# Decode attention and MLP on one core: the output projection as one load at the end, last K and V whole, w4 in five pieces

## The chip, the cores and the metric

The kernel runs on one core of a Trainium2 chip. The metric is the device time of one execution in microseconds (us). Three runs of the kernel before took 404.21, 404.23 and 404.65 us; the median is 404.23 us. Beside them one execution was profiled, and the views quoted below are of that one.

## What is computed

One token (S = 1, D = 1024) goes through two blocks that work side by side, and their sum is the output. Cut to what matters:

```
xn  = layernorm(x)
A:  q = xn @ wq                      # wq 1024 x 4096: 32 heads of 128
    scores = q . k_cache / sqrt(128) # 4 KV groups, 8 heads each, 65536 keys
    o = softmax(scores) . v_cache
    a = o.reshape(4096) @ wo         # wo 4096 x 1024
B:  h  = gelu(layernorm(xn) @ w1);  hs = shift(h) @ w2   # shifted parts: zero for S = 1 (padding)
    x1 = xn + hs
    b  = x1 + gelu(layernorm(x1) @ w3) @ w4   # w3 1024 x 3584, w4 3584 x 1024
out = x + a + b
```

With one token every shifted part of h is padding, so hs is zero; the kernel still loads w1 and w2 and multiplies by them. All inputs are bf16. The K and V caches have 67 MB each, and with the weights some 170 MB are read once.

## The kernel before

**Slots.** All large inputs go through a pool of three slots (`big`, SLOTS = 3) of 128 partitions by 32768 bf16 values, 8 MB each. The list `slots` (L105 to L117) gives the order of the work: wq; then for each of the four KV groups two rounds of K and V, each load 32768 keys of one group (8 MB), with w3 after the first round; after group 2 (counted from 0) one slot with three pieces of wo and w1; after group 3 one slot with the last piece of wo, w2 and the first 10 rows of w4; and one with the other rows of w4. The last K and the last V are loaded as two halves of 4 MB into one slot, so that the first half can be worked on while the second comes. w4's 28 rows per partition are cut into pieces of 10, 7, 5, 3, 2 and 1 (W4_PIECES, L21), each with its own load.

**Order of the loads.** `issue` (L122) starts the loads of a slot, all from SyncE's queue (L128). `ensure` is called before each slot's work with a lookahead of two, so SyncE issues slot i + 2 in its list when the slot that it takes over has been consumed; SyncE waits in order, so a load that waits holds back those behind it. Loads signal their completion on a few semaphores that they take in turn, and a load that comes to one that is still in use by an earlier load waits for that load: on SyncE the first K waits for one of the small loads of x, and the first V for wq.

**Head.** ScalarE's queue loads x twice: over partitions in four parts (x_bf, L140) and as one row in three parts (x_row_bf, L144). Two layernorms follow (`layernorm`, L193 on). Four `accx` rows of 256 (L227) put x plus its normed form, which is the rest of the sum, into the PSUM row accumulator psB by `row_acc` (L184); they are the first of what is summed there. On PE the wq product (`rows_product`, L268) stands behind the matmuls of these rows.

**Attention.** `compute_K` transposes K in 32 x 32 blocks on VectorE in place (L364, four pieces for each half) and multiplies with the queries (L368); then max, exp and the transposed probabilities (L372 to L405). `compute_V` multiplies with V (L415) and rescales the running sum og (L423). After a group's last V, `group_end` (L428 to L447) masks og, sums the heads' parts by matmuls with a selector (sel8big, L434 and L436), reduces (L439, L442) and scales it into oT5, 128 x 8, one for each group.

**Row accumulator.** psB is one PSUM bank in which four strips of the PE array (32 columns apart, by tile_position) hold four quarters of the output row, 256 values each. wo (L454), w2 and w4 are all added by `row_acc`: a one-column weight and a 256-column slice of the loaded rows as the moving side, four matmuls for each row:

```
def compute_wo(g):
    for j in range(8):
        for h4 in range(4):
            row_acc(h4, oT5[:, j:j + 1], wt[:, j, QC * h4:QC * (h4 + 1)])
```

The hidden row of w3 and that of w1 go to DRAM and back from GpSimd's queue to be laid out over partitions (`bounce`, L306). After the last w4 piece ScalarE copies psB (L351) and SyncE stores the row (L352).

Of the kernel before, what the change touches and what calls it, by code (L numbers as in the profile page):

```python
# [17 lines left out]
KEYS = 16384  # L18
HALVES = 2
LOOKAHEAD = 2  # L20
W4_PIECES = (10, 7, 5, 3, 2, 1)  # L21
# [3 lines left out]
def kernel(  # L25
# [51 lines left out]
    wo_v = A_wo.rearrange("(g p j) n -> g p (j n)", g=HKV, p=P)  # L77
# [7 lines left out]
    def source(piece):  # L85
# [9 lines left out]
        if kind == "wo":  # L95
            return wo_v[piece[1]]
# [3 lines left out]
        _, g, t, parts = piece  # L100
        cache = A_k_cache if kind == "K" else A_v_cache
        v = cache[0, g, t * BK:(t + 1) * BK, :].rearrange("(p k) d -> p (k d)", p=P)
        return v if parts is None else v[:, parts * KEYS:(parts + 1) * KEYS]

    slots = [[("wq",)]]  # L105
    for g in range(HKV):
        for t in range(BIG):
            parts = range(HALVES) if (g, t) == (HKV - 1, BIG - 1) else (None,)
            for kind in ("K", "V"):
                slots.append([(kind, g, t, h) for h in parts])  # L110
            if (g, t) == (0, 0):
                slots.append([("w3",)])
        if g == HKV - 2:
            slots.append([("wo", i) for i in range(HKV - 1)] + [("w1",)])
    n4 = len(W4_PIECES)
    slots.append([("wo", HKV - 1), ("w2",), ("w4", 0)])
    slots.append([("w4", q) for q in range(1, n4)])  # L117
# [4 lines left out]
    def issue(pieces):  # L122
        t = big.tile([P, SLOT], BF16, name="slot")
        at = 0
        for piece in pieces:
# [4 lines left out]
            if piece[0] in ("K", "V"):  # L130
                for h in range(HALVES):
                    if piece[3] in (None, h):
                        loaded[(piece[0], piece[1], HALVES * piece[2] + h)] = t[:, h * KEYS:(h + 1) * KEYS]
# [9 lines left out]
    for a, b in ((0, D // 2), (D // 2, 3 * D // 4), (3 * D // 4, D)):  # L143
        nc.scalar.dma_start(out=x_row_bf[:, a:b], in_=A_x[0, 0:1, a:b])  # L144
# [80 lines left out]
    for j in range(4):  # L225
# [14 lines left out]
    mask16 = const.tile([P, 16], F32, name="mask16")  # L240
    nc.vector.tensor_tensor(out=mask16[:], in0=sel32[:, 0:16], in1=sel32[:, 16:32], op=ALU.add)
# [3 lines left out]
    sel8big = const.tile([P, P], F32, name="sel8big")  # L245
    nc.vector.tensor_copy(out=sel8big[:].rearrange("p (hl dd) -> p hl dd", dd=16),
                          in_=sel8[:].unsqueeze(2).to_broadcast([P, 8, 16]))
# [89 lines left out]
    def compute_w2():  # L337
        wt = loaded[("w2",)].rearrange("p (c n) -> p c n", n=D)
        for c in range(DC):
            for j in range(4):  # L340
                row_acc(j, st["gT"][:, c:c + 1], wt[:, c, QC * j:QC * (j + 1)])

# [85 lines left out]
    def group_end(g, og):  # L428
# [3 lines left out]
                                in1=mask4[:].unsqueeze(2).to_broadcast([P, 4, P]), op=ALU.mult)  # L432
        pe = ps_M.tile([P, 512], F32, name="pm_e", tag="pm")
        nc.tensor.matmul(pe[:, P:P + 1], lhsT=sel8big[:], rhs=lp[:, 0:1], start=True, stop=True)  # L434
        for cg in range(4):
            nc.tensor.matmul(pe[:, 0:P], lhsT=sel8big[:], rhs=og[:, 128 * cg:128 * (cg + 1)],  # L436
                             start=(cg == 0), stop=(cg == 3), skip_group_check=True)
        msk = one.tile([P, 16, 8], F32, name="msk")
        nc.vector.tensor_tensor(out=msk[:], in0=pe[:, 0:P].rearrange("p (dd j) -> p dd j", j=8),  # L439
                                in1=mask16[:].unsqueeze(2).to_broadcast([P, 16, 8]), op=ALU.mult)  # L440
        o5 = one.tile([P, 8], F32, name="o5")
        nc.vector.tensor_reduce(out=o5[:], in_=msk[:].rearrange("p dd j -> p j dd"), axis=AX.X, op=ALU.add)  # L442
        rl = one.tile([P, 1], F32, name="rl")
        nc.vector.reciprocal(out=rl[:], in_=pe[:, P:P + 1])
        oT5 = one.tile([P, 8], BF16, name=f"oT5_{g}")
        nc.vector.tensor_scalar(out=oT5[:], in0=o5[:], scalar1=rl[:, 0:1], scalar2=None, op0=ALU.mult)
        st[("oT5", g)] = oT5  # L447

    def compute_wo(g):
# [47 lines left out]
```

## Time and profile before

| what | value |
|---|---|
| median of three runs | 404.23 us (404.21 to 404.65) |
| the profiled execution | 405.7 us |
| its span, first to last instruction | 403.9 us |
| busy: PE, DVE, ACT, POOL | 220.7, 214.2, 34.5, 6.0 us |
| instructions on all engines | 3569 |
| HBM read | 169.88 MB, 421 GB/s over the span |
| mean granted TensorE clock | 0.823 of full speed |
| K transposes (L364) | 64, 2281 ns each, 143.0 us |
| K matmuls (L368) | 512, 415 ns each by their records, 135.0 us |
| V matmuls (L415) | 512, 494 ns each by their records, 43.3 us |

PE is TensorE's matmuls, DVE is VectorE, ACT ScalarE, POOL GpSimd, and SP SyncE, which issues the loads; ACTq and SPq are the queues of those engines when they issue a DMA. A record's length overlaps with its neighbours' on PE, so the busy time of a group is less than count times mean. The chain of work that ended last is followed back from the last instruction: at each step to what released it. A slice row gives the busy share in 40 equal stretches of the span in tenths. "Landing" is the time at which all of a load has arrived.

### The profile page before, as it was taken

Reading aid. Unit: us, or ns where it says so; the run is one execution under the profiler, and the core shown is the slowest. Engines: PE = TensorE matmul, PEld = TensorE weight load, DVE = VectorE, ACT = ScalarE, POOL = GpSimd, SP = SyncE. Lnnn points to the kernel's source line nnn. Section 1 sums busy time; section 2 is a strip of 40 time slices with the busy share of each in tenths; the row PEclk is TensorE's granted clock in tenths of the full one; section 3 lists DMA queues with packets and bytes.
Section 4 is the critical chain, followed back from the end, with each engine's and each line's share of the span. In section 5 each row is a group of like instructions: output and inputs, shape, how many; then the busy total and the mean of one; then the engine's idle time right before and its main releaser. Section 6 shows DMA issues by size and latency. Waiting matters only on the chain.

```text
span 403.9 us, 3569 instructions
## 1 busy us (share of the span) xinstructions
PE 220.7 (55%) x1540; PEld 92.6 (23%) x1540; DVE 214.2 (53%) x246; ACT 34.5 (9%) x60; POOL 6.0 (1%) x17
## 2 busy tenths in 40 slices
PE   0004858640987196619663954485820676766733
PEld 0002223220332132203231421132500222222421
DVE  0003189601985598239846962796400994986200
ACT  0001000420021001100110011002100004002000
POOL 3000000000000000000000000000100000000000
PEclk9999969995696689657985998599775699899665
DMA  9999999999999999999999999999999999999993
GB/s 402 428 415 416 415 435 437 441 417 436 435 415 430 454 428 430 428 422 441 449 422 441 423 415 467 429 389 419 456 433 422 454 401 422 440 435 415 427 419 138
DMA packets 4957, 170.12 MB, mean 421 GB/s; under 512 B 833, under 2 KB 846, under 8 KB 1230
## 3 DMA queue, kind: packets, MB, share of 16 engines
q1 hardware_dynamic: 4616, 169.87, 97.9%
q8 instruction: 12, 0.20, 0.2%
q0 software_dynamic: 128, 0.02, 0.0%
q10 hardware_dynamic: 198, 0.00, 0.0%
q14 instruction: 3, 0.02, 0.0%
HBM read 169.88 MB, written 0.01 MB: 421 GB/s over the span
## 4 chain that ended last, share of the span: by engine, by line
DMA 64%; DVE 27%; PE 7%; ACT 1%; ACTq 1%; issue 0%; SPq 0%; DVEq 0%
DMA slot<-in_A_k_cache_dram 38%; DVE slot L364 22%; DMA x_row_bf<-in_A_x_dram 10%; DMA slot<-in_A_v_cache_dram 9%; DMA slot<-in_B_w_dram 7%; PE oacc L415 2%; PE sc L368 2%; DVE mx L372 2%; PE rows L268 2%; DVE pT L405 1%; ACT p_sb L391 1%; DVE qst L281 1%; ACTq L140 0%; DVE og L423 0%; PE psB L185 0%
## 5 line engine op out<-in xcount | busy, mean ns | idle before, releaser
L368 PE MATMUL sc<-slot,qst 128*128 128x512 bf16 x512 | 135.0, 415 | 92.9 <-DVE slot L364 92.6
L364 DVE STREAM_TRANSPOSE slot<-slot 128x2048 f32<-128x2048 f32 x64 | 143.0, 2281 | 59.2 <-DMA slot<-in_A_k_cache_dram 59.2
L368 PEld LDWEIGHTS <-qst 128*128 128x128 bf16 x512 | 51.6, 103 | 164.5 <-issue 51.4
L415 PE MATMUL oacc<-slot,pT 128*32 128x512 bf16 x512 | 43.3, 494 | 4.3 <-DVE pT L405 2.0
L391 ACT ACTIVATE p_sb<-sc,nm 128x1024 bf16<-128x1024 f32 x16 | 17.8, 1114 | 176.5 <-DVE nm L388 112.4
L405 DVE STREAM_TRANSPOSE pT<-p_sb 128x1024 bf16<-128x1024 bf16 x16 | 19.9, 1243 | 16.3 <-ACT p_sb L391 16.3
L372 DVE TENSOR_REDUCE mx<-sc 128x1 f32<-128x1024 f32 x16 | 19.2, 1202 | 7.4 <-PE sc L368 7.4
L423 DVE SCALAR_TENSOR_TENSOR og<-og,alpha,oacc 128x512 f32<-128x512 f32 x12 | 9.0, 747 | 24.4 <-PE oacc L415 24.4
L415 PEld LDWEIGHTS <-pT 128*32 128x32 bf16 x512 | 16.0, 116 | 23.3 <-issue 14.2
L197 PE MATMUL pm_ln<-early 128*128 128x1 f32 x4 | 1.1, 355 | 33.0 <-DVE early L233 30.5
L191 DVE CAST early<-x_bf 128x8 f32<-128x8 bf16 x1 | 0.2, 172 | 28.8 <-DMA x_bf<-in_A_x_dram 28.8
L374 PE MATMUL pm_mx<-ident_f,mx 128*1 128x128 f32 x16 | 4.3, 270 | 16.4 <-DVE mx L372 16.4
L185 PE MATMUL psB<-slot,dst_h 128*1 128x256 bf16 x112 | 7.0, 408 | 9.8 <-DMA slot<-in_B_w_dram 9.8
L391 ACT ACT_TABLE_LOAD x3 | 3.8, 1283 | 91.0 <-DVE nm L386 58.8
L197 PEld LDWEIGHTS pm_ln<-early 128*128 128x128 f32 x4 | 1.0, 312 | 33.1 <-issue 30.5
L436 PE MATMUL pm_e<-og,sel8big 128*128 128x128 f32 x32 | 4.6, 288 | 5.6 <-DVE og L430 5.6
L381 PE MATMUL pm_mx<-ident_f,rep 1*128 1x1 f32 x16 | 3.6, 223 | 7.5 <-DVE rep L378 7.5
L185 PEld LDWEIGHTS <-dst_h 128*1 128x1 bf16 x112 | 3.7, 110 | 13.3 <-issue 11.6
L268 PE MATMUL rows<-slot,early 128*32 128x512 bf16 x64 | 6.5, 592 | 0.0
L381 PEld LDWEIGHTS pm_mx<-ident_f,rep 1*128 1x128 f32 x16 | 2.2, 139 | 17.8 <-DVE rep L378 17.8
L374 PEld LDWEIGHTS pm_mx<-ident_f,mx 128*1 128x1 f32 x16 | 1.3, 79 | 21.8 <-DVE mx L372 20.8
L185 PE MATMUL psB<-accx,early 1*1 1x256 f32 x8 | 3.6, 603 | 4.2 <-DVE accx L227 4.2
(84 smaller groups left out, 85.7 us busy)
## 6 DMA issues: line engine op xcount, KB each, us to landing
slot<-in_A_wo_dram SPq DMA_DIRECT2D x4, 2048.0 KB
slot<-in_A_k_cache_dram SPq DMA_DIRECT2D x2, 4096.0 KB, 51.2
slot<-in_A_v_cache_dram SPq DMA_DIRECT2D x2, 4096.0 KB
slot<-in_B_w_dram SPq DMA_DIRECT2D x1, 7168.0 KB, 29.1
slot<-in_B_w_dram SPq DMA_DIRECT2D x2, 2048.0 KB, 42.3
slot<-in_B_w_dram SPq DMA_DIRECT2D x1, 2560.0 KB, 44.5
slot<-in_B_w_dram SPq DMA_DIRECT2D x1, 1792.0 KB, 25.3
slot<-in_B_w_dram SPq DMA_DIRECT2D x1, 1280.0 KB, 28.0
```

Source lines behind the costliest of these rows:

```text
L185: nc.tensor.matmul(psB[32 * j:32 * j + 1, :], lhsT=lhsT, rhs=rhs, start=(not row_started[j]), stop=False, tile_position=(0, 32 * j), skip_ ...
L268: nc.tensor.matmul(acc[32 * j:32 * j + 32, bk, 0:width], lhsT=xp[:, c, :], rhs=wt[:, cl, ch * width:(ch + 1) * width], start=(c == 0), sto ...
L364: nc.vector.transpose(out=kf[:, cg, :], in_=kf[:, cg, :])
L368: nc.tensor.matmul(sc[:, hf, :], lhsT=qst[:, o:o + 128], rhs=kr[:, cg, hf, :, bp // 2, :, bp % 2], start=(cg == 0 and bp == 0), stop=(cg = ...
L372: nc.vector.reduce_max(out=mx[:], in_=sc[:].rearrange("p h n -> p (h n)"), axis=AX.X)
L374: nc.tensor.transpose(pm[0:1, 0:P], mx[:, 0:1], ident_f[:])
L381: nc.tensor.transpose(pm[:, P:P + 1], rep[0:1, :], ident_f[0:1, 0:1])
L391: nc.scalar.activation(out=p_sb[:], in_=sc[:], func=ACTF.Exp, bias=nm[:, 0:1], scale=SCALE, accum_out=lb[:, 0:1])
L405: nc.vector.transpose(out=pT[:], in_=p_sb[:])
L415: nc.tensor.matmul(oacc[32 * u:32 * (u + 1), :], lhsT=pT[:, hf, 32 * t:32 * (t + 1)], rhs=vt[:, :, hf, t, :], start=(hf == 0 and t < 4), s ...
L423: nc.vector.scalar_tensor_tensor(out=st["og"][:], in0=st["og"][:], scalar=alpha[:, 0:1], in1=oacc[:], op0=ALU.mult, op1=ALU.add)
L436: nc.tensor.matmul(pe[:, 0:P], lhsT=sel8big[:], rhs=og[:, 128 * cg:128 * (cg + 1)], start=(cg == 0), stop=(cg == 3), skip_group_check=True)
```

## The change

wo, 8 MB, becomes one load in a slot of its own behind the last V, laid out so that partition p has wo's rows 32p to 32p + 31 one after the other. The attention output is laid out to match: `group_end` now writes 32 partitions by 32 values for its group into one tile oT (128 x 32) that all four groups share, with a selector of 32 columns on the group's own strip. `compute_wo` multiplies 32 columns of oT by 512 columns of wo each, 64 matmuls into a PSUM tile of its own, on four strips in turn: even and odd rows, left and right half. ScalarE copies that tile to wrow, and `add_wo`, called at the end of `compute_w2`, adds the four strips into psB by four f32 matmuls with a two-column selector (selw).

The slot after group 2 then holds w1 and w4's first piece; the slot behind wo holds w2 and the other w4 pieces. The last K and V are loaded whole like the others. w4's rows are cut into 13, 7, 5, 2 and 1. x_row comes in one load. The loads from SyncE's queue go from 32 to 26.

```diff
--- before.py
+++ after.py
@@ -18,7 +18,7 @@
 KEYS = 16384
 HALVES = 2
 LOOKAHEAD = 2
-W4_PIECES = (10, 7, 5, 3, 2, 1)
+W4_PIECES = (13, 7, 5, 2, 1)
 
 
 @with_exitstack
@@ -74,7 +74,7 @@
     w3_v = B_w3.rearrange("(p c) f -> p (c f)", c=DC)
     wq_v = A_wq.rearrange("(p c) n -> p (c n)", c=DC)
     w4_v = B_w4.rearrange("(m c) n -> m c n", c=FC)
-    wo_v = A_wo.rearrange("(g p j) n -> g p (j n)", g=HKV, p=P)
+    wo_v = A_wo.rearrange("(p j) n -> p (j n)", p=P)
     w1_v = B_w1.rearrange("(p c) n -> p (c n)", c=DC)
     w2_v = B_w2.rearrange("(m c) n -> m (c n)", c=DC)
     assert sum(W4_PIECES) == FC
@@ -93,28 +93,26 @@
         if kind == "w2":
             return w2_v
         if kind == "wo":
-            return wo_v[piece[1]]
+            return wo_v
         if kind == "w4":
             c0 = w4_start[piece[1]]
             return w4_v[:, c0:c0 + W4_PIECES[piece[1]], :].rearrange("p c n -> p (c n)")
-        _, g, t, parts = piece
+        _, g, t, _ = piece
         cache = A_k_cache if kind == "K" else A_v_cache
-        v = cache[0, g, t * BK:(t + 1) * BK, :].rearrange("(p k) d -> p (k d)", p=P)
-        return v if parts is None else v[:, parts * KEYS:(parts + 1) * KEYS]
+        return cache[0, g, t * BK:(t + 1) * BK, :].rearrange("(p k) d -> p (k d)", p=P)
 
     slots = [[("wq",)]]
     for g in range(HKV):
         for t in range(BIG):
-            parts = range(HALVES) if (g, t) == (HKV - 1, BIG - 1) else (None,)
             for kind in ("K", "V"):
-                slots.append([(kind, g, t, h) for h in parts])
+                slots.append([(kind, g, t, None)])
             if (g, t) == (0, 0):
                 slots.append([("w3",)])
         if g == HKV - 2:
-            slots.append([("wo", i) for i in range(HKV - 1)] + [("w1",)])
+            slots.append([("w1",), ("w4", 0)])
     n4 = len(W4_PIECES)
-    slots.append([("wo", HKV - 1), ("w2",), ("w4", 0)])
-    slots.append([("w4", q) for q in range(1, n4)])
+    slots.append([("wo",)])
+    slots.append([("w2",)] + [("w4", q) for q in range(1, n4)])
 
     st = {}
     loaded = {}
@@ -129,8 +127,7 @@
             loaded[piece] = t[:, at:at + w]
             if piece[0] in ("K", "V"):
                 for h in range(HALVES):
-                    if piece[3] in (None, h):
-                        loaded[(piece[0], piece[1], HALVES * piece[2] + h)] = t[:, h * KEYS:(h + 1) * KEYS]
+                    loaded[(piece[0], piece[1], HALVES * piece[2] + h)] = t[:, h * KEYS:(h + 1) * KEYS]
             at += w
         assert at <= SLOT
 
@@ -140,8 +137,7 @@
         nc.scalar.dma_start(out=x_bf[32 * a:32 * a + 32, :],
                             in_=A_x[0, 0, 32 * a * DC:(32 * a + 32) * DC].rearrange("(p c) -> p c", c=DC))
     x_row_bf = ppool.tile([1, D], BF16, name="x_row_bf", tag="p")
-    for a, b in ((0, D // 2), (D // 2, 3 * D // 4), (3 * D // 4, D)):
-        nc.scalar.dma_start(out=x_row_bf[:, a:b], in_=A_x[0, 0:1, a:b])
+    nc.scalar.dma_start(out=x_row_bf[:], in_=A_x[0, 0:1, :])
 
     n_issued = [0]
 
@@ -237,14 +233,22 @@
     nc.vector.tensor_tensor(out=sel8[:], in0=sel32[:, 0:8], in1=sel32[:, 8:16], op=ALU.add)
     nc.vector.tensor_tensor(out=sel8[:], in0=sel8[:], in1=sel32[:, 16:24], op=ALU.add)
     nc.vector.tensor_tensor(out=sel8[:], in0=sel8[:], in1=sel32[:, 24:32], op=ALU.add)
-    mask16 = const.tile([P, 16], F32, name="mask16")
-    nc.vector.tensor_tensor(out=mask16[:], in0=sel32[:, 0:16], in1=sel32[:, 16:32], op=ALU.add)
+
+    maskq = const.tile([P, 4], F32, name="maskq")
+    nc.vector.tensor_tensor(out=maskq[:], in0=sel8[:, 0:4], in1=sel8[:, 4:8], op=ALU.add)
 
     mask4 = const.tile([P, 4], F32, name="mask4")
     nc.vector.tensor_reduce(out=mask4[:], in_=sel32[:].rearrange("p (cg h) -> p cg h", h=8), axis=AX.X, op=ALU.add)
-    sel8big = const.tile([P, P], F32, name="sel8big")
-    nc.vector.tensor_copy(out=sel8big[:].rearrange("p (hl dd) -> p hl dd", dd=16),
-                          in_=sel8[:].unsqueeze(2).to_broadcast([P, 8, 16]))
+    sel8q = const.tile([P, 32], F32, name="sel8q")
+    nc.vector.tensor_copy(out=sel8q[:].rearrange("p (hl dq) -> p hl dq", dq=4),
+                          in_=sel8[:].unsqueeze(2).to_broadcast([P, 8, 4]))
+
+    selw = const.tile([P, 2], F32, name="selw")
+    for b in range(2):
+        nc.vector.tensor_tensor(out=selw[:, b:b + 1], in0=ident_f[:, 32 * b:32 * b + 1],
+                                in1=ident_f[:, 64 + 32 * b:64 + 32 * b + 1], op=ALU.add)
+
+    oT = const.tile([P, 32], BF16, name="oT")
 
     psel = tpool.tile([P, 4, P], BF16, name="psel", tag="pT")
     iv = ident_bf.rearrange("p (b i r) -> p b r i", b=2, r=2)
@@ -339,6 +343,7 @@
         for c in range(DC):
             for j in range(4):
                 row_acc(j, st["gT"][:, c:c + 1], wt[:, c, QC * j:QC * (j + 1)])
+        add_wo()
 
     def compute_w4(q):
         wt = loaded[("w4", q)].rearrange("p (c n) -> p c n", n=NOUT)
@@ -430,28 +435,41 @@
         nc.vector.tensor_tensor(out=og[:].rearrange("p (c d) -> p c d", c=4),
                                 in0=og[:].rearrange("p (c d) -> p c d", c=4),
                                 in1=mask4[:].unsqueeze(2).to_broadcast([P, 4, P]), op=ALU.mult)
+        rows = slice(32 * g, 32 * g + 32)
         pe = ps_M.tile([P, 512], F32, name="pm_e", tag="pm")
-        nc.tensor.matmul(pe[:, P:P + 1], lhsT=sel8big[:], rhs=lp[:, 0:1], start=True, stop=True)
+        nc.tensor.matmul(pe[rows, P:P + 1], lhsT=sel8q[:], rhs=lp[:, 0:1], start=True, stop=True,
+                         tile_position=(0, 32 * g), skip_group_check=True)
         for cg in range(4):
-            nc.tensor.matmul(pe[:, 0:P], lhsT=sel8big[:], rhs=og[:, 128 * cg:128 * (cg + 1)],
-                             start=(cg == 0), stop=(cg == 3), skip_group_check=True)
-        msk = one.tile([P, 16, 8], F32, name="msk")
-        nc.vector.tensor_tensor(out=msk[:], in0=pe[:, 0:P].rearrange("p (dd j) -> p dd j", j=8),
-                                in1=mask16[:].unsqueeze(2).to_broadcast([P, 16, 8]), op=ALU.mult)
-        o5 = one.tile([P, 8], F32, name="o5")
-        nc.vector.tensor_reduce(out=o5[:], in_=msk[:].rearrange("p dd j -> p j dd"), axis=AX.X, op=ALU.add)
+            nc.tensor.matmul(pe[rows, 0:P], lhsT=sel8q[:], rhs=og[:, 128 * cg:128 * (cg + 1)],
+                             start=(cg == 0), stop=(cg == 3), tile_position=(0, 32 * g), skip_group_check=True)
+        msk = one.tile([P, 4, 32], F32, name="msk")
+        nc.vector.tensor_tensor(out=msk[rows], in0=pe[rows, 0:P].rearrange("p (dq i) -> p dq i", dq=4),
+                                in1=maskq[rows, :].unsqueeze(2).to_broadcast([32, 4, 32]), op=ALU.mult)
+        o5 = one.tile([P, 32], F32, name="o5")
+        nc.vector.tensor_reduce(out=o5[rows], in_=msk[rows].rearrange("p dq i -> p i dq"), axis=AX.X, op=ALU.add)
         rl = one.tile([P, 1], F32, name="rl")
-        nc.vector.reciprocal(out=rl[:], in_=pe[:, P:P + 1])
-        oT5 = one.tile([P, 8], BF16, name=f"oT5_{g}")
-        nc.vector.tensor_scalar(out=oT5[:], in0=o5[:], scalar1=rl[:, 0:1], scalar2=None, op0=ALU.mult)
-        st[("oT5", g)] = oT5
-
-    def compute_wo(g):
-        wt = loaded[("wo", g)].rearrange("p (j n) -> p j n", n=NOUT)
-        oT5 = st.pop(("oT5", g))
-        for j in range(8):
-            for h4 in range(4):
-                row_acc(h4, oT5[:, j:j + 1], wt[:, j, QC * h4:QC * (h4 + 1)])
+        nc.vector.reciprocal(out=rl[rows], in_=pe[rows, P:P + 1])
+        nc.vector.tensor_scalar(out=oT[rows], in0=o5[rows], scalar1=rl[rows, 0:1], scalar2=None, op0=ALU.mult)
+
+    def compute_wo():
+
+        wt = loaded[("wo",)].rearrange("p (j n) -> p j n", n=NOUT)
+        psW = ps_M.tile([P, 512], F32, name="pm_w", tag="pm")
+        nc.vector.memset(psW[:], 0.0)
+        n_j = wt.shape[1]
+        for j in range(n_j):
+            for b in range(2):
+                q = 2 * (j % 2) + b
+                nc.tensor.matmul(psW[32 * q:32 * q + 1, :], lhsT=oT[:, j:j + 1], rhs=wt[:, j, 512 * b:512 * b + 512],
+                                 start=(j < 2), stop=(j >= n_j - 2), tile_position=(0, 32 * q), skip_group_check=True)
+        st["wrow"] = one.tile([P, 512], F32, name="wrow", tag="og")
+        nc.scalar.copy(out=st["wrow"][:], in_=psW[:])
+
+    def add_wo():
+        wrow = st.pop("wrow")
+        for q in range(4):
+            c0 = QC * (q % 2)
+            row_acc(q, selw[:, q // 2:q // 2 + 1], wrow[:, c0:c0 + QC])
 
     compute = {"wq": compute_wq, "w3": compute_w3, "w1": compute_w1, "w2": compute_w2, "w4": compute_w4,
                "wo": compute_wo, "K": compute_K, "V": compute_V}
@@ -460,8 +478,7 @@
         for it in pieces:
             if it[0] in ("K", "V"):
                 for h in range(HALVES):
-                    if it[3] in (None, h):
-                        compute[it[0]](it[1], HALVES * it[2] + h)
+                    compute[it[0]](it[1], HALVES * it[2] + h)
             else:
                 compute[it[0]](*it[1:])
```

## The prediction

> **What bounds the kernel now.** I read the page's slices and queues first, then the chain of work that ended last, SyncE's own timeline, and the timelines of the head and the tail.
>
> From the page:
>
> ```profile
> span 403.9 us, 3569 instructions
> ...
> DMA  9999999999999999999999999999999999999993
> ...
> q1 hardware_dynamic: 4616, 169.87, 97.9%
> q8 instruction: 12, 0.20, 0.2%
> ...
> DMA 64%; DVE 27%; PE 7%; ACT 1%; ACTq 1%; issue 0%; SPq 0%; DVEq 0%
> ```
>
> The DMA row is at nine tenths or more in every slice but the last. One queue (q1, SyncE's loads) moves 169.87 MB and fills 97.9% of 16 engines over the span. PE (55% busy) and DVE (53%) only follow. So a change is worth what it takes off the stream of loads, off the time before it starts, or off the time after its last byte. The bytes are the same after the change: wo is still 8.39 MB, and the K, V and w4 bytes are only cut differently. At most 2.1% of 403.9, some 8 us, is not streaming, and most of that is the start and the end, which the change leaves.
>
> The stream runs as long as SyncE issues ahead of it. Its timeline (start, length, engine and line, operation):
>
> ```profile
> 50.23 0.33 SPq L128 DMA_DIRECT2D slot<-in_B_w_dram  x1
> 75.06 0.33 SPq L128 DMA_DIRECT2D slot<-in_A_k_cache_dram  x1
> ...
> 276.68 0.33 SPq L128 DMA_DIRECT2D slot<-in_A_k_cache_dram  x1
> ```
>
> The DMA issues give 29.1 us from the w3 issue (50.23) to its landing, so 79.3. The K load behind it was issued at 75.06, only 4.3 us ahead. In the chain the K loads land at:
>
> ```profile
> 75.06 24.18 DMA slot<-in_A_k_cache_dram
> ...
> 131.40 46.57 DMA slot<-in_A_k_cache_dram
> ...
> 209.47 45.90 DMA slot<-in_A_k_cache_dram
> ```
>
> that is at 99.24, 177.97 and 255.37. Between the last two lie four loads of 8.39 MB: 77.40 / 4 = 19.35 us each. The K load at 75.06 took 99.24 - 79.3 = 19.9 us behind w3. **0.55 us** was lost where the queue was nearly dry.
>
> **Part 1: x_row in one load, not three.** The head:
>
> ```profile
> 39.67 0.40 DVE L227 TENSOR_SCALAR accx<-x_row_bf,early 1x256 f32<-1x256 bf16 x1 [3.33 <-DMA x_row_bf<-in_A_x_dram]
> ...
> 42.30 0.40 DVE L227 TENSOR_SCALAR accx<-x_row_bf,early 1x256 f32<-1x256 bf16 x1 [2.23 <-DMA x_row_bf<-in_A_x_dram]
> ...
> 43.70 6.46 PE L268 MATMUL rows<-slot,early 128*32 128x512 bf16 x64
> ```
>
> The first accx ran at 34.80, when the first piece was there; the second and third pieces held the last two until 39.67 and 42.30, and the 64 wq matmuls stand behind them on PE. With one load all four accx can run from about 34.8. PE's second layernorm sum ran at 36.98 to 37.56, and the remaining accx matmuls follow, so wq starts at about 38.1: 5.6 us earlier. SyncE's issue of w3 (when wq's slot is free) and of the next K follow by as much: 50.2 becomes 44.6, 75.06 becomes 69.5, 9.8 us ahead of w3's landing. Fewer ACT-queue loads also mean that the first K and V loads no longer wait for an earlier load to finish (they were issued at 10.46 and 22.63); the stream was full then, so that is worth nothing. Value: the 0.55 us above, **0 to -0.55**; I take -0.55, since the next smallest lead in this trace (the K issue at 10.46 against wq's landing 21.9 us after 0.74, 12.2 us) shows no loss and 9.8 is nearer to it.
>
> **Part 2: larger pieces of the stream.** The DMA view for 276 to 290 us (only 2 MB loads: wo and w1), then for 99 to 275 us (8 MB loads):
>
> ```profile
> q1 hardware_dynamic: 412, 5.96, 100.2%
> ```
> ```profile
> q1 hardware_dynamic: 1351, 75.61, 99.4%
> ```
>
> Per busy time, 5.96 MB / (14 us x 1.002) = 424.9 GB/s against 75.61 / (176 x 0.994) = 432.2. For wo's 8.39 MB that is 19.74 against 19.41: -0.33 us. The 4 MB halves of the last K and V (330 to 360 us: 12.85 MB at 99.6%, 430.1 GB/s) give 39.01 against 38.82 over 16.78 MB: -0.19. w4 in five pieces rather than six: one boundary less; by the 2 MB step (three boundaries for 0.33 us) that is 0.1 at most, and I count -0.03. Sum **-0.55**. The page shows why it is no more: loads overlap in the queue.
>
> The Trainium skill, "DMA: Bandwidth & Descriptors", section Bandwidth, fits each (software-queue) DMA as about 2.0 us fixed plus its bytes over 436 GB/s. Read as a price per load, six loads less would be 12 us and the forecast about 392. The 97.9% above leaves no such time between loads, so I don't use it.
>
> **Part 3: the order.** The slot behind V of group 2 carries w1 and w4's first 13 rows (5.5 MB) instead of three wo pieces and w1 (8.39 MB). V of group 2 lands at about 255.37 + 19.35 = 274.7, the slot at 274.7 + 5.5/0.428 = 287.6. The next K is issued when the K before it is consumed, at 276.68: a lead of 10.9 us where it was 17.6. It lies in the same gap between 4.3 and 12.2: cost **0 to +0.55**, taken as 0. The 52 matmuls of those rows (59 ns each as in the tail, 3.1 us) run near 288 to 291, while PE waits for K (about 306): nothing, and 3 us of PE were there before for 96 wo matmuls. Everything later comes 6.6 us earlier. The last K, now whole, lands near 345; a whole K took from 313.95 to 335.19 (21.2) and its V 7.9 more (to 343.05), the group's end 3.75 (376.79 to 380.54): oT at about 378. wo lands near 384, so the loss of the halves' early start is hidden by 6 us. The last issue (w2 and four w4 pieces, after K's slot is free) is at about 366, some 17 us ahead of wo's landing.
>
> **Part 4: the tail.** wo's matmuls now stand behind nearly all loads. The tail before:
>
> ```profile
> 380.54 1.88 PE L185 MATMUL psB<-slot,oT 128*1 128x256 bf16 x32 [1.06 <-DVE oT L446]
> ...
> 392.69 1.66 PE L185 MATMUL psB<-slot,dst_h 128*1 128x256 bf16 x28 [2.00 <-DMA slot<-in_B_w_dram]
> ...
> 395.78 1.24 PE L185 MATMUL psB<-slot,dst_h 128*1 128x256 bf16 x20 [1.42 <-DMA slot<-in_B_w_dram]
> ...
> 398.65 0.81 PE L185 MATMUL psB<-slot,dst_h 128*1 128x256 bf16 x12 [1.64 <-DMA slot<-in_B_w_dram]
> ```
>
> Seven rows came in 392.69 - 388.40 = 4.29 us: 428 GB/s. Behind wo come w2 and 15 rows, 6.03 MB: 14.1 us, plus 0.41 for the last four matmuls: a cover of 14.5. PE's work in it: 64 matmuls of 512 columns on four strips: 32 such of L415 took 1.91 to 3.60 us, so 3.8 to 7.2; w2 1.9; four f32 adds of 256 columns, by the eight accx records (603 ns each, four in 1.64) 2.9, at the most 8 x 0.603 = 4.8, at the least 1.2 (eight f32 records of pm_e, L436); w4 1.66 + 1.24 + 0.5 + 0.41 = 3.8. That is 10.7 to 17.7, so **0 to +3.2**. The granted clock was 0.50 from 388 to 404 and 1.00 in stretches before; with wo half at one and half at the other (5.5) the sum is 14.1, under the cover: I take 0.
>
> The skill's "TensorE: Matmul & The Clock Gate", Part 1, speaks against this part: an idle PE falls to half clock and needs some 3.4 us of activity to leave it. By that rule wo would cost about 5.3 us (32 matmuls at each pace), an estimate; were the whole tail slow, 7.2.
>
> **Part 5: instruction loading.** The q8 row has 12 packets of 16 KB, one of them between 395 and 398 us. In that time three rows (0.79 MB) took 398.65 - 395.78 = 2.87 us where 428 GB/s gives 1.84: **1.0 us** lost on the path. PE's instruction list, as built, shrinks from 2952 to 2825 rows, so this packet may fall away or move. Between 0 and -1.0 (a packet at a worse place: +1.0); no view says how far the next-slowest DMA engine was behind, so I take a quarter: -0.25.
>
> **Sum.** -0.55 - 0.55 + 0 + 0 - 0.25 = -1.35 us. The span becomes about 402.6. The profiled execution took 405.7 with a span of 403.9; the median of the runs is 404.23, 0.3 over the span. I apply the difference to the median: **402.9**.
>
> **Rivals.**
> - *The last instruction packet leaves the path* (the whole -1.0, and up to as much again): 404.23 - 2.1 = 402.1, down to 401.3. For it: fewer PE instructions. Against: each packet slows some engine. 16%.
> - *Nothing measurable*: the lead at the group-3 K is too short (+0.55), a packet lands worse (+0.5), or the head's 0.55 was not the dry queue: 403.6 to 404.5. 18%.
> - *PE becomes the bound of the tail* (slower): the four strips do not overlap for these one-row outputs over 512 columns. Serially, as for L368 (seven in 1.70, 0.243 each), wo takes 15.5 and the work 24.1 against 14.5: +9.6 - 1.35, so 412.5. It decides from 14.5 us of PE work on; a milder form, all at half clock with adds at 4.8, gives 404.23 - 1.35 + 3.2 = 406.1. Against: L185 and L415 place four strips and step at 59 to 60 ns with records of some 400 ns. 8%.
> - *The forecast*, 402.0 to 403.6: 58%.
>
> A measurement of this kernel can tell about 0.2%, 0.8 us, from no change; that is 403.4 here. Most of the forecast's 58% (50) and the first rival (16) lie below; 26 lie within; 8 above. The range 401.4 to 404.3 leaves out the slow rival and about a tenth at its ends.
>
> **What would show it.** Right: x_row no longer gates L227 and wq starts near 38; w3 and K issued near 44.6 and 69.5, K landing 19.35 after w3; wo landing some 14 us before the end and PE idle again before the last w4 piece; the chain's last long step a B_w load. Wrong: PE back to back from wo to the end; a K wait near 306 longer than the size gives; a q8 packet in the last 5 us with a long gap between w4 pieces.

## The result, and the profile after

| kernel | median, us | lowest to highest | profiled execution | its span |
|---|---|---|---|---|
| before | 404.28 | 404.21 to 404.65 | 405.7 | 403.9 |
| after | 402.73 | 402.64 to 402.95 | 402.64 | 400.9 |

The ratio of the medians is 0.9960, with a 95% interval of 0.9947 to 0.9973: 1.55 us less. The forecast was 402.9, and its direction holds. The spans of the two profiles differ by 3.0 us, twice as much, because before's profiled execution was a high one: most of its executions take 404.1 to 404.7 us. So a span of before is best set beside 402.5 (an execution of 404.25 less the 1.75 us that lie around the span in every kernel here), and the forecast's remark that the median is 0.3 us over the span paired two different executions.

From after's page:

```profile
span 400.9 us, 3446 instructions
...
DMA  9999999999999999999999999999999999999994
...
q1 hardware_dynamic: 3752, 169.87, 98.2%
q8 instruction: 11, 0.18, 0.2%
...
DMA 51%; DVE 33%; PE 10%; another core or an unknown queue 3%; ACT 1%; issue 1%; ACTq 0%; SPq 0%; DVEq 0%
```

The bytes are the same 169.87 MB, the stream still fills every slice, and there are 864 packets fewer, since a larger load is cut into larger packets. The q8 row, which is instruction loading, has one packet less. The kernel is bound as it was.

The head of after (start, length, engine and line, operation; in brackets the idle time before and what ended it):

```profile
37.11 0.40 DVE L223 TENSOR_SCALAR accx<-x_row_bf,early 1x256 f32<-1x256 bf16 x1 [0.23 <-PE psB L181]
...
38.50 6.41 PE L272 MATMUL rows<-slot,early 128*32 128x512 bf16 x64
```

x_row no longer gates the last accx (42.30 before), and wq starts at 38.50 (43.70 before). SyncE's timeline shows the issues that follow, and the chain of work shows when the K loads land:

```profile
44.98 0.33 SPq L126 DMA_DIRECT2D slot<-in_B_w_dram  x1
69.81 0.33 SPq L126 DMA_DIRECT2D slot<-in_A_k_cache_dram  x1
...
274.99 0.33 SPq L126 DMA_DIRECT2D slot<-in_A_k_cache_dram  x1
...
366.17 2.23 SPq L126 DMA_DIRECT2D slot<-in_B_w_dram  x5
```

```profile
69.81 28.99 DMA slot<-in_A_k_cache_dram
...
131.62 44.69 DMA slot<-in_A_k_cache_dram
...
207.69 46.06 DMA slot<-in_A_k_cache_dram
...
274.99 30.16 DMA slot<-in_A_k_cache_dram
...
367.02 28.59 DMA slot<-in_B_w_dram
```

Start and length give landings at 98.80, 176.31, 253.75, 305.15 and 395.61. w3 landed 34.5 us after its issue, at 79.5 (the time to landing in the page's list of DMA issues), so the first of these K loads came 19.3 us behind it; before it was 19.9.

The tail of after, TensorE alone, and behind it the stretches of 4 us (length, PE, PEld, DVE, ACT, POOL, granted clock, DMA share, GB/s):

```profile
383.48 6.28 PE L463 MATMUL pm_w<-slot,oT 128*1 128x512 bf16 x64 [2.17 <-DMA slot<-in_A_wo_dram]
...
389.59 1.04 PE L181 MATMUL psB<-slot,dst_g 128*1 128x256 bf16 x32
...
390.46 0.61 PE L181 MATMUL psB<-wrow,selw 128*1 128x256 f32 x8
...
392.62 0.94 PE L181 MATMUL psB<-slot,dst_h 128*1 128x256 bf16 x28 [1.54 <-DMA slot<-in_B_w_dram]
...
395.66 2.22 PE L181 MATMUL psB<-slot,dst_h 128*1 128x256 bf16 x32 [2.10 <-DMA slot<-in_B_w_dram]
```

```profile
384.00:388.00 4.00, 4.00 (x44) 1.22 (x36) 0.00 (x0) 0.00 (x0) 0.00 (x0) 0.50 1.01 431
388.00:392.00 4.00, 3.08 (x64) 1.34 (x57) 0.00 (x0) 0.59 (x1) 0.00 (x0) 0.89 0.96 404
```

PE waits for wo (2.17 us) and then twice more for w4 (1.54 and 2.10 us). The bracket behind an instruction is what tells: DMA, not PE, ends each of these waits, so the moved matmuls are hidden. At the start of wo the granted clock is 0.50; over the next 4 us it is 0.89.

So each step that the forecast listed as visible is there. Whether each is worth what the forecast put on it can't be read from two profiles, one of them of a high execution. That is what the experiments are for.

### The profile page after: what moved, and what is told of

It reads as the page before. It is cut to its first block, busy times and chain, and to the rows that moved or that the text cites. A ratio compares the mean times of both kernels' runs of the same rounds, so it can differ in the third digit from the quotient of the medians.

```text
span 400.9 us, 3446 instructions
## 1 busy us (share of the span) xinstructions
PE 217.9 (54%) x1484; PEld 89.7 (22%) x1484; DVE 215.1 (54%) x249; ACT 35.1 (9%) x61; POOL 6.0 (1%) x17
## 3 DMA queue, kind: packets, MB, share of 16 engines
q1 hardware_dynamic: 3752, 169.87, 98.2%
## 4 chain that ended last, share of the span: by engine, by line
DMA 51%; DVE 33%; PE 10%; another core or an unknown queue 3%; ACT 1%; issue 1%; ACTq 0%; SPq 0%; DVEq 0%
DMA slot<-in_A_k_cache_dram 37%; DVE slot L369 27%; DMA slot<-in_B_w_dram 7%; DMA x_bf<-in_A_x_dram 7%; PE oacc L420 4%; PE sc L373 3%; DVE mx L377 3%; PE rows L272 2%; DVE pT L410 1%; PE psB L181 1%; ACT p_sb L396 1%; DVE qst L285 0%; PE pm_mx L386 0%; DVE m L381 0%
## 5 line engine op out<-in xcount | busy, mean ns | idle before, releaser
L369 DVE STREAM_TRANSPOSE slot<-slot 128x2048 f32<-128x2048 f32 x64 | 142.9, 2280 | 65.7 <-DMA slot<-in_A_k_cache_dram 65.6
L410 DVE STREAM_TRANSPOSE pT<-p_sb 128x1024 bf16<-128x1024 bf16 x16 | 19.9, 1245 | 17.3 <-ACT p_sb L396 17.3
L377 DVE TENSOR_REDUCE mx<-sc 128x1 f32<-128x1024 f32 x16 | 19.3, 1204 | 4.5 <-PE sc L373 4.4
L443 PE MATMUL pm_e<-og,sel8q 128*32 128x128 f32 x32 | 6.0, 348 | 5.2 <-DVE og L435 5.2
L463 PE MATMUL pm_w<-slot,oT 128*1 128x512 bf16 x64 | 6.3, 577 | 2.2 <-DMA slot<-in_A_wo_dram 2.2
L181 PE MATMUL psB<-slot,dst_h 128*1 128x256 bf16 x112 | 5.4, 308 | 3.7 <-DMA slot<-in_B_w_dram 3.6
L272 PE MATMUL rows<-slot,xpad 128*32 128x448 bf16 (+1 forms) x80 | 5.8, 368 | 1.9 <-DMA slot<-in_B_w_dram 1.9
## 6 DMA issues: line engine op xcount, KB each, us to landing
slot<-in_B_w_dram SPq DMA_DIRECT2D x1, 7168.0 KB, 34.5
```

The source lines that it names most:

```text
L181: nc.tensor.matmul(psB[32 * j:32 * j + 1, :], lhsT=lhsT, rhs=rhs, start=(not row_started[j]), stop=False, tile_position=(0, 32 * j), skip_ ...
L272: nc.tensor.matmul(acc[32 * j:32 * j + 32, bk, 0:width], lhsT=xp[:, c, :], rhs=wt[:, cl, ch * width:(ch + 1) * width], start=(c == 0), sto ...
L369: nc.vector.transpose(out=kf[:, cg, :], in_=kf[:, cg, :])
L377: nc.vector.reduce_max(out=mx[:], in_=sc[:].rearrange("p h n -> p (h n)"), axis=AX.X)
L410: nc.vector.transpose(out=pT[:], in_=p_sb[:])
L443: nc.tensor.matmul(pe[rows, 0:P], lhsT=sel8q[:], rhs=og[:, 128 * cg:128 * (cg + 1)], start=(cg == 0), stop=(cg == 3), tile_position=(0, 32 ...
```

## The experiments

My first theory was the forecast itself: 0.55 us from the dry queue at x_row, 0.55 from larger pieces, 0.25 from the packet of instructions. The first rival was that one of these terms is nothing in an ordinary execution. The second came up when the parts did not add up to the whole: something that the change moves without meaning to. A table of all results first; the ratios are to the kernel before on the same chip, with their 95% intervals.

| kernel | what it is | median, us | ratio |
|---|---|---|---|
| b_xrow1 | before, x_row in one load | 404.52 | 0.9996 (0.9988 to 1.0005) |
| a_xrow3 | after, x_row in three loads | 403.11 | 0.9962 (0.9948 to 0.9975) |
| a_kv4 | after, each K and V in four loads | 404.89 | 1.0005 (0.9996 to 1.0013) |
| a_pe128 | after, 64 more matmuls in idle time | 402.97 | 0.9955 (0.9942 to 0.9967) |
| after2 | after, unaltered | 402.87 | 0.9961 (0.9947 to 0.9974) |
| b_nowo | before with all but the wo part | 404.36 | 0.9996 (0.9987 to 1.0005) |
| a_wo4 | after, wo in four loads | 403.19 | 0.9968 (0.9957 to 0.9980) |
| a_wo2x | after, wo's matmuls done twice | 402.74 | 0.9958 (0.9945 to 0.9970) |
| b_align_512 | before, slots moved in SBUF | 403.25 | 0.9974 (0.9964 to 0.9983) |
| a_off352 | after, slots moved back | 403.96 | 0.9989 (0.9980 to 0.9998) |
| a_off64 | after, slots 64 bytes on | 403.86 | 0.9986 (0.9978 to 0.9995) |
| b_nowo_align_512 | b_nowo, slots moved | 403.33 | 0.9972 (0.9961 to 0.9983) |

### x_row alone: b_xrow1 and a_xrow3

b_xrow1 does Part 1 on the kernel before; a_xrow3 undoes it in the kernel after.

```diff
-    for a, b in ((0, D // 2), (D // 2, 3 * D // 4), (3 * D // 4, D)):
-        nc.scalar.dma_start(out=x_row_bf[:, a:b], in_=A_x[0, 0:1, a:b])
+    nc.scalar.dma_start(out=x_row_bf[:], in_=A_x[0, 0:1, :])
```

> The kernel before with x_row in one load, nothing else changed (part 1 alone). Theory (the queue of loads was nearly dry when the second K load was issued at 75.06 us): w3 and that K load are issued 5 to 6 us earlier (near 45 and 70), the K load lands 19.35 us behind w3, and the time falls by 0.4 to 0.9 us to 403.4 to 403.9. Rival (the stream is full there anyway and the slow K load has another cause): the issues move but the time stays at 404.2 to 404.4.

> The changed kernel with x_row in three loads again (part 1 undone). Theory of the dry queue: the K load is issued near 75 again and lands about 19.9 us behind w3; 403.1 to 403.6 against 402.73. Rival (part 1 is worth nothing, all of the gain is in the pieces and in instruction loading): 402.6 to 402.9.

Measured: b_xrow1 404.52 beside 404.47 for before. SyncE's timeline of b_xrow1:

```profile
44.08 0.33 SPq L128 DMA_DIRECT2D slot<-in_B_w_dram  x1
68.90 0.33 SPq L128 DMA_DIRECT2D slot<-in_A_k_cache_dram  x1
```

and of a_xrow3:

```profile
49.29 0.33 SPq L126 DMA_DIRECT2D slot<-in_B_w_dram  x1
74.12 0.33 SPq L126 DMA_DIRECT2D slot<-in_A_k_cache_dram  x1
```

The issues move by 5.2 us, as they should, and the time does not follow. In a_xrow3 w3 landed 30.2 us after its issue, at 79.5; the K behind it was issued 5.4 us ahead of that and landed at 98.84, 19.3 us behind: a lead of 5.4 us costs nothing. In b_align_512, below, the lead is 4.9 us (issue at 74.70, w3 at 79.57) and the K comes 19.5 us behind. In b_xrow1, with a lead of 10.8 us, it comes 19.4 us behind. The 0.55 us that the forecast read from before's profile belongs to that one execution, with a lead of 4.3. a_xrow3 is 0.25 to 0.4 us over after, which is where the theory of the dry queue had it. But its result is ready when after's is: ScalarE copies psB at 397.97 (397.93 in after, 398.10 in after2). The difference lies behind the store, see the last section. So x_row is worth about nothing in the median.

### Cutting loads: a_kv4 and a_wo4

Both add loads of 2 MB to the kernel after, 48 over the whole stream or 3 in wo:

```diff
-            nc.sync.dma_start(out=t[:, at:at + w], in_=src)
+            cuts = 4 if piece[0] in ("K", "V") else 1        # a_wo4: == "wo"
+            for i in range(cuts):
+                nc.sync.dma_start(out=t[:, at + i * w // cuts:at + (i + 1) * w // cuts],
+                                  in_=src[:, i * w // cuts:(i + 1) * w // cuts])
```

> The changed kernel with every K and V load cut into four loads of 2 MB (64 loads in place of 16), into the same slots. Theory (a price by the size of the rows of a load, 0.33 us for each 8.39 MB in 2 MB loads, 0.11 for each further load): +16 x 0.33 = 5.3 us, 407.5 to 408.5. Rival A (about 2 us fixed for each load, paid one after another): 48 more loads, +96 us, 499. Rival B (loads in the queue cost nothing at all for being cut): 402.6 to 403.0.

> The changed kernel with wo in four loads of 2 MB (8 rows of each partition each) into the same slot, at the same place and with the same matmuls. Theory (0.045 us for each further load): +0.14, 402.8 to 403.0. Rival A (0.33 us for 8.39 MB in 2 MB loads, as forecast): 403.0 to 403.2. Rival B (the single load of wo carries the gain): 403.7 to 404.2. Rival C (the gain of wo is in its matmuls, its place or the instruction count): as the theory.

Measured: a_kv4 took 404.89, 2.0 to 2.2 us over after: 2.1 / 48 = 0.045 us for each further load, or 0.13 us where 8 MB go in four loads. The forecast had 0.33 for that. a_wo4 took 403.19, 0.3 over after2. That lies in the range of Rival A (0.33, as forecast), but the copy of psB starts at 398.19, 0.1 to 0.3 behind after2 and after, and SyncE's wait behind the store is 0.3 longer; so the larger part of the 0.3 is again that wait, and what is left agrees with the 0.13 that three loads cost by the price of a_kv4. The direction of Part 2 is right, and its six loads are worth 6 x 0.045 = 0.27 us instead of 0.55.

### The packet of instructions: a_pe128

64 small matmuls into an unread PSUM tile, ahead of w1's work where PE is idle, bring PE back to 1548 matmuls (1484 in after, 1540 before):

```diff
+        pad = ps_M.tile([P, 512], F32, name="pm_pad", tag="pm")
+        for i in range(64):
+            nc.tensor.matmul(pad[0:32, 0:32], lhsT=xpad2[:, i % DC, :], rhs=xpad2[:, i % DC, :], start=True, stop=True)
```

> The changed kernel with 64 small matmuls (32 columns, into a PSUM tile that nobody reads) ahead of the w1 product, so that PE has as many instructions as in the kernel before. PE is idle there, so their own time is hidden by both theories. Theory (a 16 KB instruction packet in the last microseconds delays the DMA engine that ends last): a twelfth packet comes back near the tail and the time rises by 0.5 to 1.5 us, 403.2 to 404.2. Rival (the number and place of instruction packets doesn't reach the end): 402.6 to 402.9.

The twelfth packet came back, and into the tail; this is the queue's row in the stretch from 394 to 398 us, which after does not have:

```profile
q8 instruction: 1, 0.02, 1.4%
```

The time is 402.97, 0.1 to 0.24 over after, and by the ratios no more at all (0.9955 beside 0.9960). a_wo2x, below, has its twelfth packet in the same stretch and takes no longer than after2. A packet in the tail is seen, and is worth nothing that this can tell from zero.

The forecast had read a loss of 1.0 us from before's profile, where the three rows behind the piece of five came in 2.87 us while such a packet was on its way. b_xrow1 has the same pieces and a packet in the same stretch, from 395 to 398 us:

```profile
q8 instruction: 1, 0.02, 2.1%
```
```profile
395.36 1.24 PE L184 MATMUL psB<-slot,dst_h 128*1 128x256 bf16 x20 [1.42 <-DMA slot<-in_B_w_dram]
397.23 0.81 PE L184 MATMUL psB<-slot,dst_h 128*1 128x256 bf16 x12 [0.63 <-DMA slot<-in_B_w_dram]
```

There the three rows came in 397.23 - 395.36 = 1.87 us, about what their bytes take at 428 GB/s (1.84). So this 1.0 us, like the 0.55 at the head, belongs to the one high execution of before, and not to the packet as such. Together they cover the 1.3 us by which that execution (405.7) lies over b_xrow1's profiled one (404.40).

### wo's place in the tail: a_wo2x

The 64 matmuls of wo are done a second time, into a PSUM tile that nobody reads:

```diff
+        psX = ps_M.tile([P, 512], F32, name="pm_x", tag="pm")
+        for j in range(n_j):
+            for b in range(2):
+                q = 2 * (j % 2) + b
+                nc.tensor.matmul(psX[32 * q:32 * q + 1, :], lhsT=oT[:, j:j + 1], rhs=wt[:, j, 512 * b:512 * b + 512],
+                                 start=(j < 2), stop=(j >= n_j - 2), tile_position=(0, 32 * q), skip_group_check=True)
```

> The changed kernel with wo's 64 matmuls done a second time into a PSUM tile that nobody reads, behind the first. Theory of the cover (PE has some 14.5 us from wo's landing to its last matmul and used 10.7 in the profile, with waits of 1.5 and 2.1 us for w4 rows): 3.9 us more at full clock, 6.3 at half; the waits take up to 3.6, so 402.7 to 403.2, up to 405.5 if the clock stays at half. Rival (wo's matmuls are on the path already): 406.6 to 409. It also brings PE's instruction count back to that of the kernel before.

```profile
383.85 5.20 PE L463 MATMUL pm_w<-slot,oT 128*1 128x512 bf16 x64 [4.87 <-DMA slot<-in_A_wo_dram]
388.88 3.62 PE L469 MATMUL pm_x<-slot,oT 128*1 128x512 bf16 x64
392.34 1.04 PE L181 MATMUL psB<-slot,dst_g 128*1 128x256 bf16 x32
393.21 0.60 PE L181 MATMUL psB<-wrow,selw 128*1 128x256 f32 x8
393.64 0.93 PE L181 MATMUL psB<-slot,dst_h 128*1 128x256 bf16 x28
395.96 0.72 PE L181 MATMUL psB<-slot,dst_h 128*1 128x256 bf16 x20 [1.39 <-DMA slot<-in_B_w_dram]
397.18 1.01 PE L181 MATMUL psB<-slot,dst_h 128*1 128x256 bf16 x12 [0.50 <-DMA slot<-in_B_w_dram]
```

402.74 beside 402.87 for after2 on the same chip: a second pass of 3.62 us costs nothing, since only the wait in front of the 28 matmuls is used up. PE as the bound of the tail, the slow rival, is out by more than 3 us of work.

### All but wo: b_nowo, and after again: after2

b_nowo is before with x_row in one load, the last K and V whole and w4 in 13, 7, 5, 2, 1 rows:

```diff
-W4_PIECES = (10, 7, 5, 3, 2, 1)
+W4_PIECES = (13, 7, 5, 2, 1)
...
-            parts = range(HALVES) if (g, t) == (HKV - 1, BIG - 1) else (None,)
+            parts = (None,)
```

> The kernel before with all of the change but wo: x_row in one load, last K and V whole, w4 in 13, 7, 5, 2 and 1 rows; wo stays in four loads at its two places with its old matmuls. Theory (pieces by the price measured by cutting all K and V loads, 0.045 us for each further load): three loads less than x_row alone, 404.52 - 0.14, so 404.3 to 404.5. Rival A (a price by the size of a load's rows, 0.10 for each halved load): 404.2 to 404.3. Rival B (the last K and V in halves are what costs, by the order or the waits around them): 402.9 to 403.4, most of the gain.

> The changed kernel unaltered, beside the experiments on the same chip, as their point of reference: 402.6 to 402.9, 1.4 to 1.7 us under those runs of the kernel before that lie at its lower level (404.2 to 404.5), 2.2 to 2.8 under those at its higher level (404.9 to 405.5).

b_nowo took 404.36 beside 404.48: next to nothing, although it has three of the six fewer loads and the x_row part (its wait behind the store is 0.9 us where before has 0.6, see the last section, so its stream may be 0.4 shorter; the copy of psB starts at 399.20, at 399.55 in b_xrow1). after2 gave 402.87, as after did. So 1.5 us seemed to lie in the wo part, in which a_wo4 had found 0.3 at most and a_wo2x nothing. What else goes with the wo part is its constants: sel8big (128 x 128 f32) becomes sel8q (128 x 32), mask16 becomes maskq. The pool of constants is allocated ahead of the slots, and in the built program the first of the three slots starts at byte 26464 of each partition before, and at 26112 after; the others follow at 65536 and 131072 bytes behind it. 26464 is 51 x 512 + 352, and 26112 is 51 x 512.

### Where the slots start: b_align_512, a_off352, a_off64

b_align_512 is before with two pools allocated first, so that the slots start at 16896 = 33 x 512. Every engine's instructions are the same, in the same order; only addresses in SBUF differ, those of the constants and small tiles too. The other two are after with a pad among the constants that nothing reads, which puts the slots at 26464, where before has them, or at 26176, 64 above a multiple of 512; the tiles behind the pad move with them.

```diff
 b_align_512
-    const = ctx.enter_context(tc.tile_pool(name="const", bufs=1))
...
-    one = ctx.enter_context(tc.tile_pool(name="one", bufs=1))
...
+    const = ctx.enter_context(tc.tile_pool(name="const", bufs=1))
+    one = ctx.enter_context(tc.tile_pool(name="one", bufs=1))
 a_off352 (a_off64: 64 in place of 352)
+    pad = const.tile([P, 352], mybir.dt.uint8, name="pad")
+    nc.gpsimd.memset(pad[:], 0)
```

> The kernel before with nothing changed but the order in which its pools are laid out, so that the three slots start at 16896 bytes in each partition (33 x 512) and not at 26464 (352 above a multiple of 512, 32 above a multiple of 64). In the changed kernel they happen to start at 26112 = 51 x 512, because its constants are smaller. Theory (the start of the slots is what made the rest of the gain, a few ns for each packet of a load): 1.0 to 1.3 us less than the kernel before, 403.1 to 403.5. Rival (the gain of the wo part is in its place, its order or its matmuls): 404.2 to 404.6.

> The changed kernel with an unused tile of 352 bytes in each partition ahead of the slots, so that they start at 26464 as in the kernel before. Theory of the start address: 0.9 to 1.3 us more, 403.7 to 404.2. Rival (wo's place, order or matmuls): 402.7 to 402.9, as without it.

> The changed kernel with an unused tile of 64 bytes ahead of the slots, so that they start 64 above a multiple of 512. If a multiple of 64 is enough: 402.7 to 402.9. If it must be a multiple of 256 or 512: 403.5 to 404.2, as with 352 bytes. Rival (the start address does nothing): 402.7 to 402.9 here and with 352 bytes.

| | slots at 352 over 512 | slots at a multiple of 512 | the move gives |
|---|---|---|---|
| without the change | 404.37 (before) | 403.25 (b_align_512) | -1.1 |
| with the change | 403.96 (a_off352) | 402.87 (after2) | -1.1 |
| the change gives | -0.4 | -0.4 | |

The four corners add up to 1.5 us, of 1.55 measured: 1.1 come with the address and 0.4 with all that the change is about. after2 ran on another chip than the other three; by the ratios to before on the same chip the corners are 1, 0.9974, 0.9989 and 0.9961, which says the same. The interval of a_off352 leaves 0.1 to 0.8 for the 0.4. At 64 above the multiple (a_off64, 403.86) the loss is nearly whole, so a start at a multiple of 64 is not enough. 128 and 256 were not tried.

Where does it show? In the chain of a_off352, to be set beside that of after above:

```profile
129.35 47.24 DMA slot<-in_A_k_cache_dram
...
209.83 44.65 DMA slot<-in_A_k_cache_dram
...
275.73 30.35 DMA slot<-in_A_k_cache_dram
...
367.90 28.78 DMA slot<-in_B_w_dram
```

These land at 176.59, 254.48, 306.08 and 396.68: 0.28, 0.73, 0.93 and 1.07 us behind after. It is no single wait; the same loads, issued in the same order, come a little slower all along. The DMA view from 99 to 275 us, where 8 MB loads run, for a_off352 and for after:

```profile
q1 hardware_dynamic: 1365, 75.84, 99.8%
```
```profile
q1 hardware_dynamic: 1375, 76.01, 99.8%
```

In the same 176 us a_off352 moves 0.17 MB less, which is 0.4 us of the stream; over all of it that would be some 0.9 us (an estimate from these two rows). Per busy time, as in Part 2 of the forecast, this stretch has 431.8 to 432.2 GB/s in the five profiles whose slots start off a multiple of 512, and 432.7 to 432.9 in the eight at one (a_kv4, with its cut loads, left out). VectorE's largest work does not show it: a K transpose takes 2280 or 2281 ns in all thirteen. So it is the loads that differ, and nearly all of their bytes go into the slots. In b_align_512 the loads of 2 MB between 276 and 290 us have

```profile
q1 hardware_dynamic: 413, 6.01, 100.6%
```

that is 6.01 MB / (14 us x 1.006) = 426.7 GB/s of busy time, against 424.9 for the same loads before. Why an aligned start is quicker no run here shows.

The Trainium skill, "DMA: Bandwidth & Descriptors", section Bandwidth (on how a descriptor splits into transactions), says of reads that a descriptor which starts off a 256-byte boundary has its first transaction begin at the boundary below, and pays for the bytes in front. What moved here is the side that is written, in SBUF. The direction agrees; no run here shows whether it is the same mechanism.

### Both together: b_nowo_align_512

b_nowo with the pools in the order of b_align_512: all of the change but wo, at aligned slots.

> All of the change but wo (x_row in one load, last K and V whole, w4 in five pieces), with the slots at 16896 bytes. Theory of the start address with the measured prices (0.3 for wo in four loads): 403.0 to 403.3, within 0.3 to 0.5 of the changed kernel without moving wo at all. Rival (wo's place, order or matmuls): 404.2 to 404.5, as all but wo was without the alignment.

403.33, as b_align_512 alone has 403.25. Beside b_nowo (404.36) it is a third pair that differs in addresses alone: -1.0. Its wait behind the store is the long one of 0.9 us (0.6 in after); without those 0.3 it would stand near 403.0, and 0.1 to 0.3 would remain for the wo part, which has three further loads less (0.13). With the same 0.3 taken off b_nowo, the parts without wo hold most of the change's 0.4 at the old addresses too: the copy of psB starts at 399.20 in b_nowo and at 399.05 in a_off352. These are single profiles and differences of 0.1 to 0.3 us, so this split is likely rather than shown.

## Why the prediction was right or wrong

The time was right, 402.9 against 402.73, and so were the direction and the bound; but its largest part came from a cause that is not in the sum. By its steps:

- **Part 1, -0.55: failed as a size; measured about 0 (b_xrow1's interval: -0.5 to +0.2).** The issues moved as foreseen (w3 at 44.98, K at 69.81). The step that failed is "0.55 us was lost where the queue was nearly dry": that is true of the profiled execution, and the forecast carried it over to the median. b_xrow1 shows no gain, and a_xrow3 no loss at a lead of 5.4 us. Where before's ordinary executions have their second K load, and with which lead, can't be seen from the one profile of it.
- **Part 2, -0.55: right in direction, twice too large.** a_kv4 prices a further load at 0.045 us, so six are 0.27. The mis-sized term is wo's 0.33, read as bytes per busy time of the DMA engines; cutting 8 MB into four measured 0.13. Busy time per byte is not the time at which the stream ends: read in the same way, from 99 to 275 us, a_kv4 has 427.7 GB/s beside 432.7 in after, which would be 3.6 us over the 134 MB of K and V. The Trainium skill's 2.0 us for each DMA of a software queue, which the forecast weighed and left aside, stands in "DMA: Bandwidth & Descriptors", section "Anatomy of one DMA", and not in Bandwidth. As a price per load it would have made a_kv4 96 us slower (an estimate by that page); it was 2.1.
- **Part 3, 0: right, with less to spare than foreseen.** The group-3 K was issued at 274.99, and the last five loads at 366.17. But oT is written at 382.08, not 378, and wo's matmuls start at 383.48 behind wo's landing: some 1.2 us are left where the forecast had 6. The last K came and was consumed as foreseen (at 344.95 and 366.17); the V work was mis-sized. From there to the last update of og it took 11.7 us (to 377.87), not 7.9. The forecast had the 7.9 from a V of before whose 32 matmuls took 1.91 us, at a granted clock of 1.00; at the end of after they take 3.60, at 0.50. The rest is the group's end, 4.4 us from the update of og to oT instead of 3.75. The V rows before and after, and the write of oT:

```profile
341.09 1.91 PE L415 MATMUL oacc<-slot,pT 128*32 128x512 bf16 x32 [0.99 <-DVE pT L405]
```
```profile
374.21 3.60 PE L420 MATMUL oacc<-slot,pT 128*32 128x512 bf16 x32 [0.79 <-DVE og L428]
...
382.08 0.24 DVE L452 TENSOR_SCALAR oT<-o,rl 32x32 bf16<-32x32 f32 x1
```

- **Part 4, 0: right.** wo took 6.28 us, in the forecast's 3.8 to 7.2; the adds 0.61, below its lower end of 1.2; the clock started at 0.50 and stood at 0.89 in the next stretch. a_wo2x shows that 3.62 us more fit into the cover. The skill's "TensorE: Matmul & The Clock Gate", Part 1, was weighed with 5.3 us for wo (an estimate); 6.28 in after and 5.20 in a_wo2x lie around it.
- **Part 5, -0.25: the event came, the price is near 0.** The packet left the tail. With it back the time is 0 to 0.24 us higher in a_pe128 and not higher in a_wo2x. The step that failed is the 1.0 us put down to the packet: b_xrow1 has the packet at the same rows and not the loss.
- **Not in the sum: -1.1 us, the start of the slots.** The smaller constants moved the slots from 352 bytes over a multiple of 512 to a multiple of it. The forecast read the diff of group_end as compute alone and did not look at what its tiles do to the addresses of those allocated behind them. b_align_512 and a_off352 show it from both sides.

So the forecast's -1.35 and the measured -1.55 agree by chance: at equal addresses the change gives about -0.4, of which the larger pieces explain 0.27 by a_kv4's price, and -1.1 was missed. Of the rivals, the one that takes the head's 0.55 out of the sum came nearest: without the address the change would have fallen within the 0.2% that it calls no change (a_off352, 0.9989). Its reason is another one, since in the profiled execution the 0.55 was lost where the forecast saw it.

Open: why the alignment matters, and from which step on below 512; what makes some executions of before, and of b_nowo too, take 404.9 to 405.6 us (the one that was profiled lost its time at two places, 0.55 us at the head and 1.0 in the tail; why it did is not known); and 0.1 to 0.2 us of the 0.4, which are no larger than the spread between the runs of one kernel. No kernel was measurably faster than the kernel after.

## What to carry to other kernels

Where a kernel is bound by one stream of loads, look up at which byte of the partition its buffers start, before and after any edit of the constants ahead of them: here, a start at a multiple of 512 was worth 1.1 us of 404, more than all of the edit's own purpose, and the order of the pools alone gives it. Take the price of a cut load from the end of the stream, not from the busy time per byte: 0.045 us for a load that is queued behind others. And before a stall in one profile is counted as gain, see whether that execution is the median's: here stalls of 0.55 and 1.0 us were not.

## What the runs showed of the hardware

- **The start of the slots**, as above: 1.0 to 1.1 us over 170 MB between a start at a multiple of 512 and starts 64 or 352 bytes above one.
- **The end of the kernel goes with the store's semaphore.** SyncE's last wait, for the store of the result to complete, is 0.6 to 0.7 us in some kernels and 0.9 to 1.0 in others. In after and in a_xrow3 (engine and line, what it waits for, us in total, times, longest):

```profile
SPq L509 <- DMA out_dram<-out: 0.6, 1, 0.6
```

```profile
SPq L510 <- DMA out_dram<-out: 1.0, 1, 1.0
```

  The store is the same in both; what differs in the built programs is which of the completion semaphores it gets, since the number of loads ahead of it differs. It is 0.9 in a_wo4, b_nowo and b_nowo_align_512, 0.7 in b_xrow1, and 0.6 in all the others, before among them. In the built programs the store has one semaphore in all kernels with 0.6, a second in the three with 0.9, a third in b_xrow1 and a fourth in a_xrow3. That it is the semaphore is inferred from this; no run changed it alone. A difference of 0.3 us between two kernels with different numbers of loads should be looked for there first.
- **The same 64 matmuls at different clocks**: wo's first pass took 6.28 us in after, where the granted clock is 0.50 from 384 to 388 us, and 5.20 in a_wo2x, where it is 0.62 there; a second pass right behind it, from 388.88 on at a clock of 1.00, took 3.62.
